# Two 64-row query matmuls side by side in the array, with slots that alternate between two blocks

## The chip, the core and the metric

The kernel runs on one core of a Trainium2 chip. The metric is the device time of one launch in microseconds (us), as the median of several runs. The core has a matmul engine (TensorE, PE in the profile; its weight loads have a row of their own, PEld), a vector engine (VectorE, DVE), an activation engine (ScalarE, ACT), a general engine (GpSimd, POOL), and a queue engine (SyncE, SP), which here issues all DMAs of the main loop. Matmuls write into PSUM, which this kernel uses as eight banks of 128 partitions by 512 fp32 columns; its other on-chip tiles lie in SBUF.

## What is computed

A transformer block on 2048 rows of 576 channels. Only the attention half touches the change:

```python
h = _layernorm(x) * (1 + ca) + sa
q = (h @ wq).reshape(B, Sq, 32, 128)          # 32 query heads
k, v = last 512 rows of the caches             # 16 key heads, each serves 2 query heads
scores = einsum("bhqd,bhkd->bhqk", q, k) * 128 ** -0.5
o = einsum("bhqk,bhkd->bhqd", softmax(scores), v)
x = x + ga * (o.reshape(B, Sq, 4096) @ wo)
...                                            # then a gated MLP of width 4608
```

`ca`, `sa` and `ga` come from a small conditioning vector. The MLP half follows the attention half on the same rows.

## The kernel before, in words

**Numbers.** Every fp32 operand of a matmul is split into an fp16 high part and an fp16 low part, and a product is the sum of three matmuls: high by high, high by low, low by high.

**Query projection.** The 576 channels are four chunks of 128 and a rest of 64. For a block of 512 rows, `hT` holds nine slices of 128 by 512: the high parts of the four chunks, the low parts of the four chunks, and in slice `2*DC` the rest, its high part in partitions 0 to 63 and its low part in partitions 64 to 127 (`modulate` writes it; GpSimd makes the low rows). The weights of the rest stand twice, one copy for each half of the partitions. So `project` needs 14 matmuls of 128 by 128 by 512: three for each chunk (line 410), and two for the rest (line 414), the high weights over all 128 rows and the low weights over all 128 rows. Of the second one only the 64 rows with the high part of `hT` matter; the other 64 add low by low.

**Slots.** The attention work is 128 slots. A slot is one query head of one block of 512 rows: `u` is the use of a key head, `j` which of its two query heads, `b` the block. Each key head is used once over all four blocks (8 slots), or twice over two blocks (4 slots each), its split operands being stored and read back. Inside a use the slots went block by block: `(b0, j0), (b0, j1), (b1, j0), (b1, j1)`.

**Order.** The program is written out by hand: each engine's queue holds its instructions in the order of the code, and nothing reorders them. A slot has four steps `t`, one for each 128 rows. In each step TensorE does the scores of the slot (three matmuls, line 483), a third of the *next* slot's query projection (`query(i + 1, t)` for t = 0, 1, 2), and one piece of the output projection (`attend_out`, six matmuls of 288 columns, line 433). After the last step come twelve matmuls for the values of the slot before (line 562). Once per slot four 128 by 128 transposes turn one tile of the softmax (line 523); the other three tiles are turned by DMA. VectorE takes the row maximum of the scores (line 487), ScalarE the exponentials (line 500) and the high halves, GpSimd the low halves. Tasks for other slots (loading, scaling and splitting the next head's weights, normalizing a block, MLP weights) are hung onto steps with `at` and `step_at`; `R` is the first step of a use.

**Output projection.** A pair of slots `(j0, j1)` of one block accumulates in PSUM tile `E`, and VectorE adds the result to the block (line 590). The eight pieces of a pair go one to a step.

**PSUM.** Tag `A` has two banks that the queries `pq` and the value sums `po` take in turn, tag `S` two for scores, `E` takes two, and tag `T` two for transposes.

Of the kernel before, what the change touches and what calls it, by code (L numbers as in the profile page):

```python
# [48 lines left out]
def tile_block(  # L49
# [30 lines left out]

    E = psum.tile([P, 2, 512], F32, tag="E", name="pe", bufs=1)
    turning = ExitStack()
    tpool = turning.enter_context(tc.tile_pool(name="tpool", bufs=2, space=PSUM))

    def t_bank():
        return tpool.tile([P, 512], F32, tag="T", name="pt")

    def half_split(a):
        return a.rearrange("p (a n) -> p a n", a=2)
# [145 lines left out]

    def turn_rows(b, m, tag):

        ps = t_bank() if tag == "T" else bank(tag, "ps_n")
        for t in range(ST):
            nc.tensor.transpose(ps[:, t * P : (t + 1) * P], norms[b][1][t][:, m * P : (m + 1) * P], ident)  # L240
        return ps

    def modulate(hT, m, ps, shift, gain, on_vector=False):

        g, s = gain[:, m : m + 1], shift[:, m : m + 1]
        hf = pool.tile([P, SB], F32, tag="hf", name="hf", bufs=HF)
        high = hT[:, m if m < DC else 2 * DC, :]
        if on_vector:
            nc.vector.tensor_scalar(hf, ps, g, s, op0=ALU.mult, op1=ALU.add)
        else:  # L250
            nc.scalar.activation(hf, ps, AF.Identity, bias=s, scale=g)
        nc.gpsimd.tensor_copy(high, hf)
        if m < DC:
            nc.gpsimd.tensor_sub(hT[:, DC + m, :], hf, high)  # L254
        else:
            nc.gpsimd.tensor_sub(high[DR:], hf[DR:], high[DR:])  # L256

    def modulate_first(hT, turned, shift, gain):

# [168 lines left out]
    def back(o, w, t, first, last):  # L428

        rows = slice(t * P, (t + 1) * P)  # L430
        for n, (x, y) in enumerate(((0, 0), (0, 1), (1, 0))):
            for h in range(2):
# [5 lines left out]
                    stop=last and n == 2,  # L438
                )

    QP = (range(0, 5), range(5, 10), range(10, 14))

# [1 line left out]
    uses = [(g, (p, p + 1), p == 0) for p in (0, 2) for g in range(FIRST)]  # L446
    uses += [(g, tuple(range(NSB)), True) for g in range(FIRST, HKV - TAIL)]
    uses += [(g, (p, p + 1), p == 0) for p in (0, 2) for g in range(HKV - TAIL, HKV)]
    slots = [(u, j, b) for u, (_, blocks, _) in enumerate(uses) for b in blocks for j in range(2)]
    begins = [next(i for i, slot in enumerate(slots) if slot[0] == u) for u in range(len(uses))]  # L450
    n = len(slots)
    state = [dict() for _ in range(n)]
# [2 lines left out]
    def query(i, part):  # L455
        u, j, b = slots[i]
        st = state[i]
        if part == 0 or i == 0:
            st["q"] = bank("A", "pq") if i else E[:, 0, :]
        ps = st["q"]  # L460
        if i == 0:
            project_first(ps, wqs[u, j], hT[b])
        else:
            project(ps, wqs[u, j], hT[b], QP[part])
        if part == len(QP) - 1:
            q = st["qT"] = pool.tile([P, 2, SB], F16, tag=("qh", "ql")[i % 2], name="qT", bufs=QB)
            nc.scalar.activation(q[:, 0], ps, AF.Copy, scale=Q_DOWN)
            if not i:
                query_low(i)
# [84 lines left out]
    def values(i):  # L554
        u, j, b = slots[i]
        st = state[i]
        v = vals[u]
        pt = st["pt"]
        po = bank("A", "po")
        for c in range(KC):  # L560
            for n, (x, y) in enumerate(((0, 0), (1, 0), (0, 1))):
                nc.tensor.matmul(  # L562
                    po, v[:, x, c, :], pt[:, y, c, :], start=c == 0 and n == 0, stop=c == KC - 1 and n == 2
                )
        st["po"] = po
# [16 lines left out]
        nc.gpsimd.tensor_sub(o[:, 1, :], on, o[:, 0, :])  # L582

    def attend_out(pair, t, j, total):
        u, _, b = slots[2 * pair]
        back(state[2 * pair + j]["o"], wos[u][:, j], t, j == 0, j == 1)
        if j == 1:
            run(*total)
            a = half_split(acc[b][:, t, :])
            nc.vector.scalar_tensor_tensor(  # L590
                a, E[:, :, :HALF], factors[:, uses[u][0], 2:3], a, op0=ALU.mult, op1=ALU.add
            )


    outs = {}
    for pair in range(n // 2):
        for k in range(2 * ST):
            if pair < n // 2 - 2:
                when = divmod((2 * pair + 4) * ST + 2 + k, ST)
            elif pair < n // 2 - 1:  # L600
                when = (n, 2 + k // 4)
            else:
                when = (n + 1, 1 + k // 3)
            outs.setdefault(when, []).append((pair, *divmod(k, 2)))

# [14 lines left out]
    def store_h(b, m, tag, tag_out):  # L622

        if m == 0:
            hd[b] = dram.tile([D, SB], F32, name=f"h{b}")
        n = P if m < DC else DR
        ps = turn_rows(b, m, tag)
        hf = pool.tile([P, SB], F32, tag=tag_out, name="hf", bufs=RB if tag_out == "raw" else HF)
        nc.scalar.activation(
            hf, ps, AF.Identity, bias=vecs["shift", "b"][:, m : m + 1], scale=vecs["gain", "b"][:, m : m + 1]  # L630
        )
        store_later(hd[b][m * P : m * P + n, :], hf[:n], ("s", b, m) if tag == "T" else None)

    def combine_tiles(pair):

# [354 lines left out]
    def mlp():  # L990

        for g in range(len(groups)):
# [12 lines left out]
                act_steps(g, -1)  # L1005
            for k, name in enumerate(ORDER):
                if name == "p1":
                    st["y"] = bank("A", "py")
                elif name in ("p2", "p7"):
                    st["x"] = bank("S", "px")  # L1010
                product(
# [242 lines left out]
    def step_at(step, task, *args):  # L1254
        at(step // ST, step % ST, task, *args)

    again = {g for g, _, whole in uses if not whole}
    for u, (g, blocks, whole) in enumerate(uses):
        R = ST * begins[u]
        if not whole:  # L1260
            step_at(R - 10, load_made, "k", u, keys)
            step_at(R - 9, load_made, "w", u, wqs, 0)
            step_at(R - 8, load_made, "w", u, wqs, 1)
            step_at(R - 5, load_made, "v", u, vals)
            step_at(R + 5, load_made, "o", u, wos)
            continue
        if u:
            A = dict(load=-22, keys=-17, wq=-13, total=-9, scale=-9, put=-8, turn=-5, vals=-1)
            if u == 1:
                A.update(load=-16, keys=-13, wq=-13)  # L1270
            A = {k: R + v for k, v in A.items()}
            step_at(A["load"], load, keys, u, load_kv, k_cache, g)
            for j in range(2):
                step_at(A["load"] + 3 + j if u > 1 else A["load"], load, wqs, (u, j), load_in, wq, 2 * g + j)
                step_at(A["wq"] + 2 * j, find, wqs, u, j, j)
                step_at(A["put"] + 4 * j, put_in, u, j)
            step_at(A["load"] + 2, load, vals, u, load_kv, v_cache, g)
            step_at(A["keys"], find, keys, u, 2)
            step_at(A["keys"] + 2, find, vals, u, 3)
            step_sum(A["total"], totals, taken, u, 0, 4)  # L1280
            step_at(A["scale"], find_scales, u, 0, 4)
            step_at(A["turn"] - 1, put_keys, u)
            step_at(A["turn"], put_keys_low, u)
            step_at(A["vals"] - 1, put_values, u)
            step_at(A["vals"], put_values_low, u)
            step_at(R - 1, load, wos, u, load_out, g)
        step_at(R + 3 if u else 9, find, wos, u, 4)
        step_sum(R + 5 if u else 11, totals, taken, u, 4, 5)
        step_at(R + 7 if u else 11, find_scales, u, 4, 5)
        for j in range(2):  # L1290
            step_at(R + 5 + j if u else 9 + j, gate_out, u, j)
            step_at(R + 11 + 2 * j if u else 12 + 2 * j, put_out, u, j)
        if g in again:
            K = max(R - 2, 5)
            step_at(K, keep_made, "k", u, keys)
            step_at(K, keep_made, "w", u, wqs, 0)
            step_at(K + 2, keep_made, "w", u, wqs, 1)
            step_at(K + 3, keep_made, "v", u, vals)
            step_at(R + 15, keep_made, "o", u, wos)


    last_group = len(groups) - 1
# [93 lines left out]
    def begin_h(b):  # L1396
        hT[b] = new_h()

    def make_h(b, m, on_vector=False):
        modulate(hT[b], m, turn_rows(b, m, "T"), vecs["shift", "a"], vecs["gain", "a"], on_vector)  # L1400

    def statistics(i, b, steps):
        for t in range(ST):
# [10 lines left out]
            statistics(i + 2 * k, b + k, 2)  # L1414
    for i, b in ((7, 2), (9, 3), (111, 0), (111, 1)):
        at(i, -1, norm_root, b)
    for i, b in ((7, 2), (10, 3)):
        norm(i, b)
        at(i + 1, 0, begin_h, b)
        for m in range(DC + 1):  # L1420
            at(i + 1 + m // 3, m % 3, make_h, b, m)


    parts = {}
# [9 lines left out]

    for b, i in ((0, 111), (1, 114)):
        norm(i, b)
        for m in range(DC + 1):
            at(i + 1 + m // 3, m % 3, store_h, b, m, "T", "raw")
            step_at(ST * (i + 1 + m // 3) + m % 3 + 1, store_now, ("s", b, m))
    at(117, -1, begin_parts, 0)  # L1440
    for c in range(3):
        i = 117 + 3 * c
# [12 lines left out]
    for b, g in ((2, 6), (3, 9)):  # L1455
# [1 line left out]
        for t in range(ST):  # L1457
            at(("m", g), t, norm_rows, b, t)
        for m in range(DC + 1):
            at(("m", g + 1 + m // 3), 2 * (m % 3), store_h, b, m, "AS"[m % 2], "raw")  # L1460
    at(("m", 12), -1, begin_parts, 1)
    for c in range(3):
        g = 12 + 6 * c
# [25 lines left out]
    at(106, 2, make_cols, "shift", "b", 3, 0.0, "T")  # L1489
    at(109, 2, make_cols, "gain", "b", 4, 1.0, "T")  # L1490
    at(109, 3, lambda: spread_peaks("b", mlp_small))
    at(110, 1, lambda: scale_cols("b", t_bank(), mlp_small, 2.0**-8))
    at(n - 3, 1, act_factors, 0, (NF - FEW) // 2)
    for b in (2, 3):
        for t in range(ST):
# [17 lines left out]
    norm_shifts(0)  # L1513
    for t in (0, 2, 1, 3):
        norm_rows(0, t)
    turned = [turn_rows(0, m, "TTAAS"[m]) for m in range(DC + 1)]
    for m in range(DC + 1):
        weigh_col(wms[0], 0, m, m < 2)
    for k, key in enumerate((wqs[0, 0], wqs[0, 1], keys[0])):
# [30 lines left out]
        at(0, t // 2, norm_rows, 1, t)  # L1550
    at(0, 2, begin_h, 1)
    for m in range(DC + 1):
        at(*((0, 2), (0, 3), (1, -1), (1, 0), (1, 1))[m], make_h, 1, m, m % 2 == 1)
    for d, step in enumerate((5, 6, 7, 4, 5)):
        step_at(step, weigh, 2, d)

# [122 lines left out]
```

## Time and profile before

| | |
|---|---|
| three runs | 2770.61 us (median), 2769.95, 2776.88 |
| profiled execution | 2773.59 us, span 2771.7 us |
| attention slots 0 to 127 | from 33.1 us; the last slot starts at 1577.4 us |
| TensorE busy | 2692.8 us (97%) |
| VectorE, ScalarE, GpSimd busy | 1999.8, 1617.5, 1881.9 us |

The span is the time from the first to the last instruction of that one execution; the remaining 1.9 us lie around it. A matmul's row in the trace gives its start and a modelled end, which lies behind the start of the next matmul, since they overlap in the pipeline; so what a matmul costs in a stream is the distance between two starts, and not its duration.

### The profile page before, as it was taken

Reading aid. Unit: us, or ns where it says so; the run is one execution under the profiler, and the core shown is the slowest. Engines: PE = TensorE matmul, PEld = TensorE weight load, DVE = VectorE, ACT = ScalarE, POOL = GpSimd, SP = SyncE. Lnnn points to the kernel's source line nnn. Section 1 sums busy time; section 2 is a strip of 40 time slices with the busy share of each in tenths; the row PEclk is TensorE's granted clock in tenths of the full one; section 3 lists DMA queues with packets and bytes.
Section 4 is the critical chain, followed back from the end, with each engine's and each line's share of the span. In section 5 each row is a group of like instructions: output and inputs, shape, how many; then the busy total and the mean of one; then the engine's idle time right before and its main releaser. Section 6 shows DMA issues by size and latency. Waiting matters only on the chain.

```text
span 2771.7 us, 44752 instructions
## 1 busy us (share of the span) xinstructions
PE 2692.8 (97%) x15406; PEld 1515.9 (55%) x15406; DVE 1999.8 (72%) x3555; ACT 1617.5 (58%) x3013; POOL 1881.9 (68%) x1748
## 2 busy tenths in 40 slices
PE   6899999999999999999999999999999999999998
PEld 3455555555555555555555555555555555555554
DVE  7877787877788787877876667777776666666666
ACT  5777778777777778787677634544443333333332
POOL 5578788888788877777669537688873465333435
PEclk8999999999999999999999999999999999999999
DMA  5778888788787788979889935656643434333332
GB/s 184 174 174 195 196 177 192 169 184 192 160 185 167 191 186 201 206 182 213 184 190 223 239 112 171 200 170 199 213 135 108 160 121 128 104 103 111 104 110 78
DMA packets 593460, 463.84 MB, mean 167 GB/s; under 512 B 442704, under 2 KB 472528, under 8 KB 592208
## 3 DMA queue, kind: packets, MB, share of 16 engines
q1 hardware_dynamic: 592944, 460.69, 64.9%
q8 instruction: 121, 1.98, 0.3%
q14 instruction: 107, 0.88, 0.1%
q10 hardware_dynamic: 288, 0.30, 0.0%
HBM read 264.19 MB, written 95.99 MB: 130 GB/s over the span
## 4 chain that ended last, share of the span: by engine, by line
PE 52%; DVE 2%; issue 1%; ACT 1%; POOL 1%; DMA 0%; SPq 0%; DVEq 0%; ACTq 0%; POOLq 0%
PE py L847 15%; PE px L847 11%; PE pe L932 7%; PE pf L932 7%; PE pe L433 3%; PE po L562 3%; PE pss L483 3%; PE pq L410 2%; PE pt L523 0%; PE pq L414 0%; DVE table L487 0%; DVE acc L590 0%; DVE on L571 0%; DMA r<-row 0%; ACT p L500 0%
## 5 line engine op out<-in xcount | busy, mean ns | idle before, releaser
L537 POOL TENSOR_TENSOR hp<-p,hp 128x512 f16<-128x512 f32 x384 | 450.2, 1175 | 271.0 <-ACT hp L532 147.9
L500 ACT ACTIVATE p<-pss,table,factors 128x512 f32<-128x512 f32 x512 | 396.9, 775 | 360.9 <-DVE table L488 186.6
L847 PEld LDWEIGHTS <-wset 128*128 128x128 f16 x3528 | 344.6, 98 | 337.9 <-issue 5.3
L487 DVE TENSOR_REDUCE table<-pss 128x1 f32<-128x512 f32 x512 | 350.3, 684 | 209.9 <-PE pss L483 205.9
L847 PE MATMUL py<-hset,wset 128*128 128x512 f16 x2016 | 483.6, 380 | 0.0
L433 PE MATMUL pe<-o 128*128 128x288 f16 x3072 | 459.6, 286 | 15.8 <-DVE acc L590 15.3
L483 PE MATMUL pss<-k,qT 128*128 128x512 f16 x1536 | 420.1, 381 | 13.7 <-ACT p L500 10.3
L433 PEld LDWEIGHTS <-o 128*128 128x128 f16 x3072 | 300.7, 98 | 189.6 <-issue 22.4
L562 PE MATMUL po<-ptw,v 128*128 128x512 f16 x1536 | 359.3, 382 | 10.4 <-DVE ptw L552 5.5
L847 PE MATMUL px<-hset,wset 128*128 128x512 f16 x1512 | 361.6, 379 | 1.6 <-ACT p L500 1.6
L410 PE MATMUL pq<-hT,wq 128*128 128x512 f16 x1092 | 283.2, 382 | 1.0 <-POOL hT L254 0.7
L94 POOL TENSOR_TENSOR akv<-u,akv 128x512 f16<-128x512 f32 x141 | 165.0, 1180 | 174.3 <-ACT akv L93 166.5
L532 ACT CAST hp<-p 128x512 f16<-128x512 f32 x384 | 237.3, 618 | 13.2 <-POOL hT L256 0.6
L562 PEld LDWEIGHTS <-v 128*128 128x128 f16 x1536 | 148.2, 98 | 175.4 <-issue 19.4
L932 PEld LDWEIGHTS <-akv 128*128 128x128 f16 x1728 | 169.6, 98 | 93.8 <-issue 4.8
L483 PEld LDWEIGHTS <-qT 128*128 128x128 f16 x1536 | 147.9, 98 | 129.0 <-issue 15.6
L590 DVE SCALAR_TENSOR_TENSOR acc<-pe,factors,acc 128x576 f32<-128x576 f32 x256 | 207.7, 811 | 10.4 <-PE pe L433 10.4
L582 POOL TENSOR_TENSOR o<-on,o 128x512 f16<-128x512 f32 x128 | 150.4, 1175 | 55.6 <-ACT o L581 52.7
L410 PEld LDWEIGHTS <-wq 128*128 128x128 f16 x1092 | 107.5, 98 | 129.7 <-issue 4.6
L926 DVE SCALAR_TENSOR_TENSOR acc<-pf,table,acc 128x576 f32<-128x576 f32 x140 | 113.4, 810 | 80.3 <-PE pf L932 80.3
L1027 ACT COPY u<-py 128x512 f32<-128x512 f32 x72 | 42.2, 586 | 202.1 <-PE py L847 200.2
L1020 ACT ACTIVATE s<-s,table 128x512 f32<-128x512 f32 x72 | 52.0, 722 | 173.9 <-DVE s L1019 173.9
(244 smaller groups left out, 4791.2 us busy)
## 6 DMA issues: line engine op xcount, KB each, us to landing
wset<-wd SPq DMA_DIRECT2D x213, 320.0 KB, 3.2
r<-row SPq DMA_DIRECT2D x128, 256.0 KB, 3.9
oset<-od SPq DMA_DIRECT2D x106, 288.0 KB, 3.2
wraw<-in_w SPq DMA_DIRECT2D x36, 768.0 KB, 5.7
wd<-wmade SPq DMA_DIRECT2D x75, 320.0 KB, 3.3
wset<-wd SPq DMA_DIRECT2D x71, 160.0 KB, 2.3
w2raw<-in_w SPq DMA_DIRECT2D x19, 576.0 KB, 5.3
wd<-ring SPq DMA_DIRECT2D x33, 320.0 KB, 2.8
```

The lines of the kernel that those rows point to most:

```text
L94: eng.tensor_sub(halves[:, 1], src, halves[:, 0])
L410: nc.tensor.matmul(ps, w[:, k // 2, m, :], hT[:, DC + m if k == 1 else m, :], start=s == 0, stop=False)
L433: nc.tensor.matmul(E[:, h, :HALF], o[:, x, rows], w[:, y, h * HALF : (h + 1) * HALF], start=first and n == 0, stop=last and n == 2,)
L483: nc.tensor.matmul(pss, q[:, x, rows], k[:, y, :], start=n == 0, stop=n == 2)
L487: nc.vector.tensor_reduce(nm[:, 0:1], pss, axis=AX.X, op=ALU.max, negate=True)
L500: nc.scalar.activation(p, pss, AF.Exp, bias=nm[:, 1:2], scale=factor, accum_out=st["l"][:, t : t + 1])
L532: nc.scalar.copy(hp[:, 0, :], state[i]["p", t])
L537: nc.gpsimd.tensor_sub(hp[:, 1, :], state[i].pop(("p", t)), hp[:, 0, :])
L562: nc.tensor.matmul(po, v[:, x, c, :], pt[:, y, c, :], start=c == 0 and n == 0, stop=c == KC - 1 and n == 2)
L590: nc.vector.scalar_tensor_tensor(a, E[:, :, :HALF], factors[:, uses[u][0], 2:3], a, op0=ALU.mult, op1=ALU.add)
L847: nc.tensor.matmul(ps, w[:, a, :], h[:, b, :], start=start and n == 0, stop=stop and n == 6, skip_group_check=True)
L932: nc.tensor.matmul(ps[:, h, :HALF], a[:, rows], w[:, b, :], start=m == 0, stop=m == 2)
```

## The change

The slots of a use now alternate between two blocks, `(b0, j0), (b1, j0), (b0, j1), (b1, j1)`, except in the first and the last use. So two consecutive slots, an even one and the odd one behind it, share the query head, and with it the weights. Blocks with odd numbers keep the low part of the rest in partitions 0 to 63 and the high part in 64 to 127, the other way round than even blocks. At the first step of the even slot's projection stand two matmuls of 64 rows: low weights, rows 0 to 63, with the even block's high part, into the even slot's bank; and low weights, rows 64 to 127, with the odd block's high part, into the odd slot's bank. Each of the two projections then needs 13 more matmuls. Queries get two banks of their own (tag `Q`); the value sums get one (tag `A`), and transposes keep one (tag `T`). The tasks that use `T` are placed anew and some go to `A`. The output projection of a pair now takes slots `i` and `i + 2`, and starts one slot later; loading and scaling the output weights moves back by 4 to 8 steps.

```diff
-    tpool = turning.enter_context(tc.tile_pool(name="tpool", bufs=2, space=PSUM))
+    tpool = turning.enter_context(tc.tile_pool(name="tpool", bufs=1, space=PSUM))
...
-            nc.gpsimd.tensor_sub(high[DR:], hf[DR:], high[DR:])
+            nc.gpsimd.tensor_sub(high[low], hf[low], high[low])
...
+    def project_paired(ps, w, hT, steps):
+        for s in steps:
+            m, k = divmod(s, 3)
+            if m < DC:
+                nc.tensor.matmul(
+                    ps, w[:, k // 2, m, :], hT[:, DC + m if k == 1 else m, :], start=False, stop=False
+                )
+            else:
+                nc.tensor.matmul(ps, w[:, 0, DC, :], hT[:, 2 * DC, :], start=False, stop=True)
...
+    PAIRED = (range(0, 4), range(4, 9), range(9, 13)), (range(0, 5), range(5, 9), range(9, 13))
...
+            quad = [(u, j, b) for j in range(2) for b in two]
+            slots += quad if 0 < u < len(uses) - 1 else [quad[k] for k in (0, 2, 1, 3)]
...
         elif not paired[i]:
             project(ps, wqs[u, j], hT[b], QP[part])
         else:
+            if i % 2 == 0 and part == 0:
+                other = state[i + 1]["q"] = bank("Q", "pq")
+                for to, rows, block in ((ps, slice(0, DR), b), (other, slice(DR, P), slots[i + 1][2])):
+                    nc.tensor.matmul(
+                        to, wqs[u, j][rows, 1, DC, :], hT[block][rows, 2 * DC, :], start=True, stop=False
+                    )
+            project_paired(ps, wqs[u, j], hT[b], PAIRED[i % 2][part])
...
-        po = bank("A", "po")
+        po = t_bank("A")
...
+        both = (i - i % 4 + pair % 2, i - i % 4 + pair % 2 + 2) if paired[i] else (i, i + 1)
...
+            elif pair == n // 2 - 3:
+                when = divmod((n - 1) * ST + 2 + k // 2, ST)
             else:
-                when = (n + 1, 1 + k // 3)
+                when = divmod((i + (5 if paired[i] else 4)) * ST + 2 + k, ST)
...
-            step_at(R - 1, load, wos, u, load_out, g)
-        step_at(R + 3 if u else 9, find, wos, u, 4)
+            step_at(R + 7, load, wos, u, load_out, g)
+        step_at(R + 10 if u else 9, find, wos, u, 4)
...
+    TIMES = (0, 2, "T"), (0, 2, "A"), (0, 3, "T"), (1, 2, "T"), (1, 3, "T")
+    for i, b in ((8, 2), (10, 3)):
+        at(i, 2, begin_h, b)
+        for m, (slot, t, tag) in zip((DC, *range(DC)), TIMES):
+            at(i + slot, t, make_h, b, m, False, tag)
```

Three places show how TensorE's and SyncE's queues change. The names carry buffer numbers: `pq` is a query bank, `hT_378` and `hT_512` are blocks 0 and 1, `wq` the query weights. First, TensorE in slot 33, behind the third matmul of the first step's scores. Before:

```order
L483 MATMUL pss_5112<-k_4791,qT_5058 128x512
L410 LDWEIGHTS wq_4719
L410 MATMUL pq_5125<-hT_512,wq_4719 128x512
...
L410 MATMUL pq_5125<-hT_512,wq_4719 128x512
L414 LDWEIGHTS wq_4719
L414 MATMUL pq_5125<-hT_512,wq_4719 128x512
L414 LDWEIGHTS wq_4719
L414 MATMUL pq_5125<-hT_512,wq_4719 128x512
L433 LDWEIGHTS o_4806
```

and with the change:

```order
L508 MATMUL pss_5083<-k_4765,qT_5030 128x512
L486 LDWEIGHTS wq_4835
L486 MATMUL pq_5096<-hT_378,wq_4835 128x512
L486 LDWEIGHTS wq_4835
L486 MATMUL pq_5097<-hT_512,wq_4835 128x512
L446 LDWEIGHTS wq_4835
L446 MATMUL pq_5096<-hT_378,wq_4835 128x512
...
L446 MATMUL pq_5096<-hT_378,wq_4835 128x512
L450 LDWEIGHTS wq_4835
L450 MATMUL pq_5096<-hT_378,wq_4835 128x512
L433 LDWEIGHTS o_4780
```

The two matmuls of line 414 at the end of the projection become one (line 450), and two 64-row matmuls into two banks (line 486) stand at its head, once for two slots. In the whole program 254 matmuls of line 414 become 14, and 120 of line 450 and 120 of line 486 (60 pairs) appear.

Second, TensorE at the third step of slot 8, where the rows of block 2 are turned for its `hT` (line 240, `pt` is a transpose bank). Before:

```order
L414 MATMUL pq_1520<-hT_378,wq_1372 128x512
L433 LDWEIGHTS o_1316
L433 MATMUL pe_76<-o_1326,o_1316 128x288
...
L240 MATMUL pt_1622<-ident_71,xn_1382 128x128
L240 MATMUL pt_1622<-ident_71,xn_1385 128x128
L240 MATMUL pt_1622<-ident_71,xn_1428 128x128
L240 MATMUL pt_1622<-ident_71,xn_1463 128x128
L483 LDWEIGHTS qT_1449
```

and with the change:

```order
L450 MATMUL pq_1351<-hT_512,wq_1223 128x512
L240 MATMUL pt_1594<-ident_71,xn_1375 128x128
...
L240 MATMUL pt_1594<-ident_71,xn_1458 128x128
L240 MATMUL pt_1603<-ident_71,xn_1375 128x128
...
L240 MATMUL pt_1603<-ident_71,xn_1458 128x128
L508 LDWEIGHTS qT_1444
```

Two tiles are turned in this step now, one into the single bank of `T` and one into that of `A`, and no piece of the output projection stands ahead of them: the paired slots start their output projection one slot later, so four steps here have none, and the last slots have two pieces in a step instead.

Third, SyncE at the first use that goes over all four blocks (first slot 24), where the output weights are loaded (`oraw`). Before:

```order
L513 DMA r_4930<-row30_4883 128x512
L544 DMA_TRANSPOSE ptw_4900<-hp_4879 128x8x128
L349 DMA oraw_4953<-in_wo 128x1152
L544 DMA_TRANSPOSE ptw_4900<-hp_4911 128x8x128
L719 DMA od21_155<-omade_4897 128x576
L510 DMA row31_5018<-l_4840 128x4
```

and with the change:

```order
L535 DMA row32_5134<-l_4950 128x4
L749 DMA od23_157<-omade_5038 128x1152
L569 DMA_TRANSPOSE ptw_5149<-hp_5092 128x8x128
L538 DMA r_5180<-row32_5134 128x512
L569 DMA_TRANSPOSE ptw_5149<-hp_5130 128x8x128
L349 DMA oraw_5202<-in_wo 128x1152
L749 DMA wd6_116<-wmade_5110 128x1280
L569 DMA_TRANSPOSE ptw_5149<-hp_5160 128x8x128
```

The load stands two slots later, between the same kinds of neighbours.

## Prediction before the run

> **What bounds the kernel now.** I read the page first, then the busy times of the attention stage, the groups of TensorE by form, the timeline of one slot, and TensorE's waits in that stage.
>
> ```profile
> span 2771.7 us, 44752 instructions
> PE 2692.8 (97%) x15406; PEld 1515.9 (55%) x15406; DVE 1999.8 (72%) x3555; ACT 1617.5 (58%) x3013; POOL 1881.9 (68%) x1748
> 33.10:1577.40 1544.30, 1501.46 (x8526) 837.80 (x8527) 1195.16 (x2424) 1158.17 (x2246) 1213.36 (x1150) 0.99 0.82 186
> ```
>
> The third row is the attention stage; its columns are length, then busy time (and count) of PE, PEld, DVE, ACT, POOL, then granted clock and DMA. TensorE is busy for 97% of it, the next engine, GpSimd, for 79%. A slot without waits looks like this on TensorE:
>
> ```profile
> 712.59 0.59 PE L410 MATMUL pq<-hT,wq 128*128 128x512 f16 x2
> 713.02 0.59 PE L414 MATMUL pq<-hT,wq 128*128 128x512 f16 x2
> 713.45 0.90 PE L433 MATMUL pe<-o 128*128 128x288 f16 x6
> 714.19 0.81 PE L483 MATMUL pss<-k,qT 128*128 128x512 f16 x3
> ...
> 724.17 0.59 PE L410 MATMUL pq<-hT,wq 128*128 128x512 f16 x2
> ```
>
> Two matmuls of line 414 take from 713.02 to 713.45, so one takes 0.216 in the stream (0.43 / 2, and 0.65 / 3 for the scores). A piece of output projection takes 0.74. The slot takes 724.17 - 712.59 = 11.58 us, and that is 38 matmuls at 0.216 (8.21), four pieces at 0.74 (2.96) and four transposes: no idle time is left in it. So a matmul taken away here is taken off the path. What the stage loses beyond this are single waits:
>
> ```profile
> PE pe L433 <- DVE acc L590: 10.5, 10, 2.4
> PE pss L483 <- ACT p L500: 10.3, 15, 2.5
> PE po L562 <- DVE ptw L552: 5.5, 8, 2.9
> PE pq L414 <- POOL hT L256: 3.5, 1, 3.5
> PE pt L240 <- ACT hf L251: 2.1, 1, 2.1
> ```
>
> (total us, times, longest). They sum to 32 us in 1544, and none belongs to a resource that the change frees.
>
> **The matmuls taken away.** A pair of slots had four matmuls of line 414, 4 x 0.216. It now has two of them and a pair of 64-row matmuls. There are 60 such pairs (120 of the 128 slots). If the two halves overlap completely, a pair of slots saves up to 0.216, 60 x 0.216 = 13.0 us. What the halves cost is nowhere in the trace for 64 rows. The nearest thing is line 169, which twice uses the array in two halves of 64 columns, with full-size matmuls ahead and behind:
>
> ```profile
> 1363.07 0.25 PE L169 MATMUL pt<-ones,wm 128*128 128x1 f32 x1
> 1363.24 0.13 PEld L169 LDWEIGHTS pt<-ones,wm 128*64 128x64 f32 x1
> 1363.25 0.23 PE L169 MATMUL pt<-ones,wm 128*64 128x1 f32 x2
> 1363.46 0.20 PE L169 MATMUL pt<-ones,wm 128*64 128x1 f32 x1
> 1363.58 0.10 PEld L483 LDWEIGHTS <-qT 128*128 128x128 f16 x1
> 1363.59 0.39 PE L483 MATMUL pss<-k,qT 128*128 128x512 f16 x1
> ```
>
> These are the last full-size matmul, the first half-array weight load, the first two half-array matmuls, then the last half-array matmul, and the first full-size load and matmul behind it. Three things are to be seen. Two half-array matmuls fit into 0.23 where one takes 0.20, so the second starts within 0.03 of the first: halves do overlap at the start, and I charge 0.03 for the pair. On the way in, the new load starts at 1363.24, which is 0.08 before the modelled end of the old matmul (1363.07 + 0.25); on the way out at 1363.58, again 0.08 before the modelled end (1363.46 + 0.20). And the matmul starts 0.01 behind its load. In a normal stream the load runs ahead, with the matmul before:
>
> ```profile
> 712.59 0.10 PEld L410 LDWEIGHTS <-wq 128*128 128x128 f16 x1
> L414 PE MATMUL pq<-hT,wq 128*128 128x512 f16 x182 | 54.2, 379 | 3.5 <-POOL hT L256 3.5
> ```
>
> (the first matmul of line 410 also starts at 712.59, and its duration is the 0.379 that line 414's row shows.) So I read the switch as: the first load of the other shape waits until the array is nearly empty.
>
> **The price of a switch.** A matmul of 512 columns has its modelled end 0.379 behind its start. The load then starts at 0.379 - 0.08 = 0.30, its matmul at 0.31, where the stream would have gone on at 0.216: 0.094 lost. A pair of slots has two switches, in behind the scores' third matmul, out ahead of the next full projection matmul; on the way out the matmul takes 0.39 and not 0.38, 0.01 more for weights that come late. Sum for a pair of slots: 0.094 + 0.216 + 0.03 + 0.094 + 0.01 = 0.444, against 2 x 0.216 = 0.432 for the two matmuls replaced. That is +0.012, and 60 x 0.012 = **+0.7 us**: the gain is spent on the two switches.
>
> The bounds. From below: the same rows also allow that the load only waits for the previous load (1363.04 + 0.19 by the row below), which in the stream would long be over; then nothing is lost, and a pair saves 0.432 - 0.246 = 0.186, 60 x 0.186 = -11.2 us.
>
> ```profile
> 1363.04 0.19 PEld L169 LDWEIGHTS pt<-ones,wm 128*128 128x128 f32 x1
> 1362.73 0.47 PE L169 MATMUL pt<-ones,wm 128*128 128x1 f32 x3
> ```
>
> From above: the load waits for the modelled end, and its matmul for the whole load of 0.10: 0.379 + 0.10 - 0.216 = 0.263 a switch, 0.526 + 0.246 - 0.432 = 0.340 a pair, +20.4 us. I take the value in the middle, since the three full-size matmuls of the second row stand about 0.11 apart ((0.47 - 0.25) / 2) while each of their loads lasts 0.19, so a load as such doesn't wait for the previous one to end; what ends together with the wait, at both switches, is the matmul.
>
> The Trainium skill, "TensorE: Matmul & The Clock Gate", Part 3 (Packing small matmuls), gives the span of packed matmuls as one matmul plus about 4 ns for each further tile and names no cost of a switch; by it a pair would save 0.432 - 0.220, an estimate of -12.7 us in all. The same skill, "TensorEngine Tiling (Array Packing)", Tiling Modes, Key Properties, speaks against the change: changing the tiling mode, not just the tile, drains the engine. The 0.08 above agrees with that second rule twice; no row here shows a switch behind a 512-column matmul.
>
> **Order of slots, output projection.** All matmuls, maxima, exponentials and GpSimd subtractions of a slot stay, only for another block. The output projection's start moves back by one slot, so four steps in slots 8 and 9 have no piece and two later slots have double; 4 x 0.74 = 3.0 us of TensorE move from there to slots 127 and 128.
>
> ```profile
> 140.90:153.90 13.00, 13.00 (x79) 7.78 (x78) 11.75 (x24) 10.72 (x22) 10.31 (x12) 1.00 1.02 243
> 153.90:166.40 12.50, 12.50 (x76) 7.45 (x75) 9.40 (x21) 10.61 (x19) 9.09 (x10) 1.00 0.67 120
> ```
>
> In slots 8 and 9 VectorE is busy for 11.75 of 13.00, so slot 8 can't get shorter by more than about 1.3; at the end the full 3.0 are added where the MLP's matmuls already fill TensorE. Bounds 0 to +1.7, I take +0.5.
>
> **Banks.** The queries took every second bank of `A`, the value sums the other; with two and one of their own neither waits more. One bank for transposes is enough for the one tile a slot, which VectorE has read by the third step. The two blocks that are normalized early, and the two at slots 111 to 118, put ten more tiles through each pair of `T` and `A`; now each must wait for ScalarE's read of the one before. The row of line 240 above has one such wait of 2.1. Each new tile has at least a step, some 2.9 us, between; where two follow in one step they go to different banks. Bounds 0 and ten waits of 0.3, +3; I take +0.5. Block 3's rest, which was made five steps before its first reader, is now read two steps (5.8 us) behind: in slot 1, with one step, that cost the 3.5 of GpSimd's `hT`; I take +0.3 of 0 to 3.5.
>
> **Output weights.** They were loaded four steps before VectorE's maximum (line 305), now three.
>
> ```profile
> 339.27 0.58 SPq L349 DMA_DIRECT2D oraw<-in_wo  x1
> 347.72 1.34 DVE L305 TENSOR_REDUCE top<-oraw 128x1 bf16<-128x1152 f32 x1
> DMA to landing us min/median/max: 4.1/5.7/9.0
> 581.70 1.05 DVE L571 TENSOR_TENSOR on<-po,r 128x512 f32<-128x512 f32 x1 [2.95 <-DMA r<-row]
> 583.53 0.90 PE L433 MATMUL pe<-o 128*128 128x288 f16 x6 [2.44 <-DVE acc L590]
> ```
>
> The shortest distance is 347.72 - 339.27 = 8.45; less a step of 2.9 it is 5.55, just under the median landing of 5.7. Behind the waiting maximum stand the scores' maxima, and behind these the exponentials and TensorE's score banks; the last two rows show that a VectorE wait of 2.95 on a DMA costs TensorE 2.44. Most uses have two or three us more in hand. Bounds 0 and 15 loads x (9.0 - 5.55) x 2.44 / 2.95 = 43 us if every load were as slow as the slowest; near the median it is nothing, and I take +0.2. The other moved tasks (gates, splits on ScalarE and GpSimd) keep their distance to the first reader: it moved by a slot, too.
>
> **Sum.** 0.7 + 0.5 + 0.5 + 0.3 + 0.2 = +2.2 us on 2773.59, the profiled execution (span 2771.7 plus 1.9). That one lies 3.0 above the median of 2770.61, inside the three runs, so the forecast is 2770.6 + 2.2 = **2773 us**, no change. A measurement of this kernel can tell 0.3%, 8.3 us, from none.
>
> **Rivals.**
> *The switch is free.* The new load needs only the earlier load, and both halves stream together: -11.2 + 1.5 for the side costs, 2761 us. For it: the halves' starts within 0.03, and loads that run a whole matmul ahead everywhere else. Against it: 0.08 before the matmul's end, twice. It is decided by the loss of a switch: below 0.02 each, the kernel is faster by more than 8.3.
> *The switch empties the array completely.* The mechanism is the one of the forecast, with the load only behind the modelled end: between 0.163 (0.379 - 0.216) and 0.263 a switch, so +0.140 to +0.340 a pair, +8.4 to +20.4 us, and 2781 to 2793 with the side costs. For it: single-column matmuls can't show what 512 columns leave in the pipeline. Against it: the 0.08. From 0.162 a switch on, the kernel is slower by more than 8.3.
> *The halves don't overlap.* They start together, but one streams behind the other: 0.186 more for a pair, +11.2, 2784 us. For it: the half-array matmuls in the trace have one column, so nothing of their streaming is seen. If the switch were free as well, nothing at all would change, 2772.
>
> **Chances.** Forecast 0.50 (its own range 2768 to 2780), free switch 0.22, empty array 0.16, halves that don't overlap 0.06, half-free switches the rest, 0.06. Of the last I count 0.05 as faster: faster 0.27, slower 0.16 + 0.05 = 0.21, the rest within 0.3%, 0.52. The range reaches down to the free switch (2759) and up over the lower part of the other two (2785).
>
> **What the profile after would show.** The two line 486 matmuls start within 0.03 of each other, the first 0.31 behind the third score matmul before it, and the next projection matmul 0.31 behind the second; two undisturbed slots together take 2 x 11.58 us, within 0.02. At 0.22 and 0.22 the free switch is right (22.97 for two slots); at 0.38 or more the empty array; a matmul behind the pair at 0.52 means no overlap. Waits of line 240 on ScalarE and of line 305 on `oraw` stay under 1 us each. The forecast is wrong above all if a 512-column matmul leaves the array otherwise than a one-column one.

## The result, and the profile after

| | before | changed |
|---|---|---|
| median | 2771.71 us | 2801.57 us |
| profiled span | 2771.7 us | 2800.9 us |
| ratio | | 1.0101, 95% interval 1.0086 to 1.0117 |

The change makes the kernel 1.0% slower, some 28 us by the ratio (29.9 by the medians, 29.2 by the profiled spans), where no change was forecast. From the page of the changed kernel, with the attention stage in the third row:

```profile
span 2800.9 us, 44829 instructions
PE 2699.5 (96%) x15406; PEld 1506.6 (54%) x15406; DVE 2001.4 (71%) x3555; ACT 1618.8 (58%) x3013; POOL 1881.6 (67%) x1748
33.10:1605.10 1572.00, 1505.83 (x8502) 825.96 (x8503) 1195.09 (x2422) 1159.70 (x2246) 1213.61 (x1150) 0.99 0.81 183
```

The engines' work is the same to a few us. The attention stage is taken up to the start of the last slot, as in the prediction: 1572.0 us where it had 1544.3. So 27.7 of the 29 us are lost in attention. There TensorE's idle time (length less busy time) grew from 42.8 to 66.2 us and its busy time by 4.4. The busy time hides the start of each wait: a 512-column matmul counts as busy up to its modelled end, 0.379 behind its start, where in the stream the next one starts at 0.216, so a wait behind it shows only from 0.163 on.

First the place that the prediction was about, a pair of 64-row matmuls in slot 63 (PE, then its weight loads):

```profile
812.56 0.81 PE L508 MATMUL pss<-k,qT 128*128 128x512 f16 x3
813.31 0.39 PE L486 MATMUL pq<-hT,wq 64*128 64x512 f16 x2
813.63 1.04 PE L446 MATMUL pq<-hT,wq 128*128 128x512 f16 x4
...
813.30 0.10 PEld L486 LDWEIGHTS <-wq 64*128 64x128 f16 x2 [0.42 <-issue]
813.62 0.33 PEld L446 LDWEIGHTS <-wq 128*128 128x128 f16 x3 [0.23 <-issue]
```

Two half matmuls fit into 0.39, no longer than one takes (0.386): they overlap fully, 0.003 to 0.004 apart in the instructions' own start times. The third score matmul starts at 812.56 + 2 x 0.216 = 812.99, the pair 0.31 behind it, and the next full matmul 0.32 behind the pair. The brackets show the weight loads that no longer run ahead. Over all 60 pairs the distance from the last score matmul to the next projection matmul is 0.633 to 0.645, 0.634 in the median, and 0.011 more follow because the weights come late, against 3 x 0.216 = 0.648 before: at this place nothing is gained and nothing lost, as forecast.

The pairs do leave their mark on the slots. Line 450 ends the projection that runs in a slot:

```profile
819.43 0.38 PE L450 MATMUL pq<-hT,wq 128*128 128x512 f16 x1
...
830.84 0.38 PE L450 MATMUL pq<-hT,wq 128*128 128x512 f16 x1
```

Undisturbed slots are no longer 11.58 us each, but in turn 11.79 (the one with the pair) and 11.36 to 11.41 (here 830.84 - 819.43, with two short matmuls of another task in it), together 23.15 without such tasks.

Now the idle time. TensorE's longest waits in the attention stage after:

```profile
PE pt L587 <- DVE ptw L577: 10.7, 17, 2.9
PE pe L310 <- DVE top L305: 9.5, 13, 1.6
PE pss L508 <- ACT p L525: 9.5, 13, 2.3
PE pe L433 <- DVE acc L616: 8.5, 6, 3.4
PE pt L240 <- DVE ptw L577: 7.4, 8, 2.3
...
PE pt L169 <- issue: 1.7, 1, 1.7
PE pt L1107 <- DVE ptw L577: 1.4, 1, 1.4
...
PE pt L169 <- DVE ptw L577: 1.2, 1, 1.2
```

and the same two releasers before:

```profile
PE pe L310 <- DVE top L305: 0.5, 1, 0.5
...
PE pt L240 <- DVE ptw L552: 0.2, 1, 0.2
```

Lines 508 and 433 wait no longer than before. New are two waits that the kernel before hardly knew. One is line 310, TensorE's column sum of the output weights' peaks, for VectorE's maximum (0.5 to 9.5). The other is whatever goes into the single transpose bank (lines 240, 169, 1107), for VectorE's read of the softmax tile in it (0.2 to 11.7, with line 169's 1.7 that ends in the same place). The value matmuls' wait for VectorE grew from 5.5 to 10.7. (Counted from start to start, so with the part that the busy time hides, line 310 lost 11.6 us to VectorE and line 240 8.7; these are the numbers in the expectations of e1 and e2.)

How the first comes about is seen in slot 34, on TensorE and then on VectorE:

```profile
471.21 0.81 PE L508 MATMUL pss<-k,qT 128*128 128x512 f16 x3
471.86 0.90 PE L433 MATMUL pe<-o 128*128 128x288 f16 x6
473.57 0.16 PE L310 MATMUL pe<-top,peak_cols 128*128 128x1 bf16 x1 [0.82 <-DVE top L305]
...
471.58 0.68 DVE L577 TENSOR_TENSOR ptw<-pt,ptw 128x512 f16<-128x512 f32 x1
472.17 1.34 DVE L305 TENSOR_REDUCE top<-oraw 128x1 bf16<-128x1152 f32 x1
473.43 0.68 DVE L512 TENSOR_REDUCE table<-pss 128x1 f32<-128x512 f32 x1
```

The maximum is hung onto a slot's third step, the sum onto the fourth. In its third step VectorE first has the softmax tile (line 577). In its fourth step TensorE has no query projection: between the scores and the sum stand only six short matmuls, so it arrives early. And the second in slot 8, where two tiles for block 2 are turned:

```profile
146.93 0.38 PE L450 MATMUL pq<-hT,wq 128*128 128x512 f16 x1
149.48 1.06 PE L240 MATMUL pt<-ident,xn 128*128 128x128 f32 x8 [2.17 <-DVE ptw L577]
...
147.79 0.64 DVE L512 TENSOR_REDUCE table<-pss 128x1 f32<-128x512 f32 x1
148.47 0.21 DVE L513 TENSOR_SCALAR table<-table,factors 128x1 f32<-128x1 f32 x1
148.64 0.69 DVE L577 TENSOR_TENSOR ptw<-pt,ptw 128x512 f16<-128x512 f32 x1
```

The tile of line 240 needs the bank that VectorE reads with line 577 in the *same* step, behind the row maximum. TensorE stands still until that read ends.

### The profile page after: what moved, and what is told of

Read it like the earlier page. It is cut to its first block, busy times and chain, and to the rows that moved or that the text cites. A ratio compares the mean times of both kernels' runs of the same rounds, so it can differ in the third digit from the quotient of the medians.

```text
span 2800.9 us, 44829 instructions
## 1 busy us (share of the span) xinstructions
PE 2699.5 (96%) x15406; PEld 1506.6 (54%) x15406; DVE 2001.4 (71%) x3555; ACT 1618.8 (58%) x3013; POOL 1881.6 (67%) x1748
## 5 line engine op out<-in xcount | busy, mean ns | idle before, releaser
L587 PE MATMUL pt<-ptw,v 128*128 128x512 f16 x1536 | 358.7, 381 | 14.9 <-DVE ptw L577 10.7
L446 PE MATMUL pq<-hT,wq 128*128 128x512 f16 x1056 | 271.5, 379 | 0.0
L446 PEld LDWEIGHTS <-wq 128*128 128x128 f16 x1056 | 99.7, 98 | 124.1 <-issue 10.0
```

The source lines that it names most:

```text
L446: nc.tensor.matmul(ps, w[:, k // 2, m, :], hT[:, DC + m if k == 1 else m, :], start=False, stop=False)
L587: nc.tensor.matmul(po, v[:, x, c, :], pt[:, y, c, :], start=c == 0 and n == 0, stop=c == KC - 1 and n == 2)
```

## The experiments

Theory A: the switch is neutral, and the loss is made of new waits around it. Theory B: the 64-row pairs themselves are the loss. Later a theory C: the new order of slots costs by itself. Every ratio is to executions of the kernel before that were taken beside that run (medians 2771.7 to 2774.0 us), so runs are compared by their ratios.

**e1, the sum later.**

```diff
-        step_sum(R + 11 if u else 11, totals, taken, u, 4, 5)
+        step_sum(R + 13 if u else 11, totals, taken, u, 4, 5)
```

> One edit of the changed kernel: TensorE's column sum of the output weights' peaks (line 310) stands at step R + 13 and no longer at R + 11, so three steps and not one behind VectorE's maximum (line 305), as far as its scales allow. Theory A (the loss is made of new waits; the switch of shapes costs nothing in sum): TensorE waited 11.6 us for that maximum over the whole trace, against 0.7 before, so the time falls by 9 to 12 us, to about 2791. Theory B (the loss comes with the 64-row pairs themselves): within 3 us of the changed kernel, 2801.

Measured: 2795.52 us, ratio to before 1.0079 (1.0066 to 1.0091), so 6 us less than the changed kernel. The wait of line 310 is gone; the waits of line 433 for VectorE grew by some 2 us. Less than forecast, but against B.

**e2, the extra tiles off the transpose bank.**

```diff
-    TIMES = (0, 2, "T"), (0, 2, "A"), (0, 3, "T"), (1, 2, "T"), (1, 3, "T")
+    TIMES = (0, 2, "A"), (0, 3, "T"), (1, -1, "T"), (1, 2, "A"), (1, 3, "T")
...
-    at(106, 2, make_cols, "shift", "b", 3, 0.0, "T")
+    at(106, 2, make_cols, "shift", "b", 3, 0.0, "A")
```

(and the same for the other two tasks of lines 169 and 1107)

> The changed kernel, with the extra tiles that were put into the single bank of T at the third step of a slot moved: at the third step they go to A's bank, into T only at the fourth step or at the slot's start. Theory A: TensorE's waits for VectorE's read of the softmax tile in that bank (8.7 us in line 240, 4.7 in lines 169 and 1107, against 0.2 before) go, so the time falls by 9 to 13 us, to about 2790. Theory B: within 3 us of 2801.

Measured: 2795.87 us, ratio 1.0084 (1.0070 to 1.0098), 5 to 6 us less. Only half of the gain, and the trace tells why:

```profile
PE pt L587 <- ACT hf L659: 2.5, 4, 1.0
PE pt L587 <- ACT hf L251: 2.3, 3, 1.4
...
PE pt L240 <- DVE ptw L577: 1.1, 1, 1.1
```

Line 240's wait fell from 7.4 to 1.1, but the tile now stands in the bank of the value sums, and the value matmuls at the slot's end wait for ScalarE to read it. In both places that were tried, the one bank of its kind was still in use.

**e3, both edits.**

> Both edits, the sum moved and the tiles moved. Theory A: the two gains add up, 18 to 25 us, to 2777 to 2784; what is left above the kernel before is the longer wait of the value matmuls for VectorE (5.5 us more than before). Theory B: still about 2800.

Measured: 2789.27 us, ratio 1.0054 (1.0040 to 1.0068): 12 to 13 us less than the changed kernel, about the sum of e1 and e2, and short of the forecast. In its trace the value matmuls wait 11.9 us for VectorE and 5.9 for ScalarE's read of the tiles, where the changed kernel had 10.7 and nothing.

**e4, full-size query matmuls.**

```diff
-        elif not paired[i]:
+        elif True:
             project(ps, wqs[u, j], hT[b], QP[part])
```

> The changed kernel with its slot order, its banks and all moved tasks, but every query projection with 14 full-size matmuls again; only the 64-row pairs are gone. Theory A: the pair and its two switches cost 0.633 us where two full matmuls and the one ahead take 0.648, so the time stays within 3 us of 2801. Theory B: the pairs are the loss, and the time falls to that of the kernel before, about 2772.

Measured: 2795.09 us, ratio 1.0085 (1.0070 to 1.0099). Against the changed kernel's 1.0101 that is 0.16%, some 4 us, where A expected at most 3 and B 29. B has fallen: of the 1.0%, 0.85% stay without any 64-row matmul. That the pairs aren't quite free either is suggested and not shown, since the two intervals overlap.

**e5, the second gate multiplication in a first step** (on top of e3).

```diff
-            step_at(R + 12 + j if u else 9 + j, gate_out, u, j)
+            step_at(R + 12 + 4 * j if u else 9 + j, gate_out, u, j)
```

> Both edits of e3, and VectorE's second multiplication of the output weights by the gate moved from step R + 13, where VectorE also normalizes a slot, to R + 16, the first step of the next slot. Theory A says that what e3 still loses is value matmuls that wait for a late VectorE (11.9 us in the attention stage, 5.5 before); this takes 0.9 us of VectorE out of the slot where the wait recurs in every use of eight slots: 2 to 5 us less than e3. A rival, that these waits come from DMAs or from ScalarE: no change against e3.

Measured: 2782.81 us, ratio 1.0041 (1.0028 to 1.0054). That is 0.13% or 4 us less than e3, as forecast, and the wait of the value matmuls for VectorE fell from 11.9 to 8.2. But the intervals of e3 and e5 overlap, and the two profiled executions are equally long (2787.5 and 2787.4 us): in e5's, the scores' wait for ScalarE's `qT` grew from 1.1 to 3.5. The gain is not shown.

**e6, a gap of one step in the kernel before.**

```diff
-        step_at(R + 3 if u else 9, find, wos, u, 4)
+        step_at(R + 4 if u else 9, find, wos, u, 4)
```

> The kernel before with one number changed: VectorE's maximum of the output weights stands at step R + 4 instead of R + 3, so one step ahead of TensorE's sum and not two, as in the changed kernel. Nothing else of the change. Theory A: TensorE waits for it in most of the 15 uses, 8 to 12 us more than before, about 2783. If the wait was only the meeting of all moved tasks: under 3 us more.

Measured: 2768.93 us, ratio 0.9988 (0.9980 to 0.9997). A miss: one step between maximum and sum costs nothing between a slot's first and second step. Line 310 waits 0.5 us there, as before. So it isn't the distance alone. (This kernel, one number away from the kernel before, is the fastest of all here, by 0.1%.)

**f1, the same gap between the third and the fourth step.** The kernel before with

```diff
-        step_at(R + 3 if u else 9, find, wos, u, 4)
+        step_at(R + 6 if u else 9, find, wos, u, 4)
-        step_sum(R + 5 if u else 11, totals, taken, u, 4, 5)
+        step_sum(R + 7 if u else 11, totals, taken, u, 4, 5)
```

and the gates at R + 8 and R + 9.

> The kernel before, with VectorE's maximum of the output weights at R + 6 and TensorE's sum at R + 7 (the third and the fourth step of a slot, one step apart, as R + 10 and R + 11 in the changed kernel), and the two gate multiplications moved behind, to R + 8 and R + 9. e6 showed that one step apart is harmless between the first and the second step. If it is the fourth step that matters, which has no query projection on TensorE, behind a third step in which VectorE also has the softmax tile: 7 to 11 us more than before, 2781. If not: within 3 us of before.

Measured: 2779.73 us, ratio 1.0029 (1.0018 to 1.0040), 8 us more than before, with nothing else of the change. The wait is the one of the changed kernel:

```profile
PE pe L310 <- DVE top L305: 9.2, 8, 2.6
```

So the place is the cause: the maximum in the third step, the sum in the fourth. Which of the two steps matters more, f1 doesn't tell. The gates moved as well here; f2 below moves them to R + 8 and R + 12 without loss. The profiled execution is the fastest of seven (2775.96 us): line 310 waits 8.7 us more in it than before, and other waits are shorter, so its span is only 2.4 us longer.

**e7, full-size matmuls and the old banks** (against e4).

```diff
-    tpool = turning.enter_context(tc.tile_pool(name="tpool", bufs=1, space=PSUM))
+    tpool = turning.enter_context(tc.tile_pool(name="tpool", bufs=2, space=PSUM))
...
-        return psum.tile([P, 512], F32, tag=tag, name=name)
+        return psum.tile([P, 512], F32, tag="A" if tag == "Q" else tag, name=name)
...
-        po = t_bank("A")
+        po = bank("A", "po")
```

> As e4 (slot order and moved tasks of the changed kernel, full-size query matmuls), with the banks of the kernel before: queries and values take two banks in turn, transposes have two. Against e4 only the banks differ. Theory A: the waits of lines 240, 169 and 1107 for VectorE's read of the single bank go, 9 to 13 us less than e4's 2795, about 2784. Theory C (it is the new order of slots that costs, whatever the banks): as e4.

Measured: 2782.91 us, ratio 1.0037 (1.0023 to 1.0051) against e4's 1.0085: 13 us. The banks alone are nearly half of the loss. The single-bank waits shrank, from 10.4 us in e4 (lines 240, 169 and 1107) to 2.4, and what e4 had of line 310's stayed:

```profile
PE pe L310 <- DVE top L305: 7.3, 8, 1.6
...
PE pt L240 <- DVE ptw L577: 2.4, 2, 1.5
```

**g1, the order alone.** e7 with the sum at R + 13 and the second gate at R + 16, so neither pairs nor fewer banks nor the sum in the fourth step.

> e7 (slot order and moved tasks of the changed kernel, full-size query matmuls, banks of the kernel before) with the sum at R + 13 and the second gate multiplication at R + 16. What is left of the change is the alternating order of the slots, the output projection one slot later, and tasks at other steps. If the bank, the sum and the pairs are the whole loss: within 4 us of the kernel before, 2773. If the order costs by itself: 8 us more, 2781 or above.

Measured: 2776.84 us, ratio 1.0011 (1.0002 to 1.0020). Theory C is worth 3 us (0.6 to 5.5 by the interval), with the tasks that moved in it.

**e8, e3 with full-size matmuls.**

> As e3 (sum moved, tiles moved), with full-size query matmuls in place of the 64-row pairs. Theory A with a switch that costs nothing: within 3 us of e3, 2789. If the unequal slots that the pairs make (11.36 and 11.79 us where all had 11.58) uncover waits, as e4 against the changed kernel suggests: 4 to 7 us less, 2784.

Measured: 2780.86 us, ratio 1.0032 (1.0020 to 1.0045), against e3's 1.0054: 6 us less. Again the kernel with pairs is 4 to 6 us slower, which their own matmuls don't show. The intervals touch here, too; two comparisons with the same sign make a cost of the pairs likely.

**f3, equal slots.** e5, and one full matmul of the even slot's projection moved into the fourth step of the lighter slot ahead:

```diff
+    def query_early(i):
+        u, j, b = slots[i]
+        st = state[i]
+        st["q"] = bank("Q", "pq")
+        st["early"] = True
+        nc.tensor.matmul(st["q"], wqs[u, j][:, 0, 0, :], hT[b][:, 0, :], start=True, stop=False)
...
+            if t == ST - 1 and i % 2 == 0 and 4 < i + 2 < n and paired[i + 2]:
+                query_early(i + 2)
```

> e5 (paired; sum, tiles and second gate moved), with one full matmul of an even slot's projection issued a slot earlier, in the fourth step of the lighter slot. So all slots take the same 11.58 us of TensorE, and the fourth step has one matmul more ahead of the value matmuls. If the unequal slots are what the pairs cost (e4 and e8 were 6 and 8 us below their paired partners): 4 to 7 us less than e5, about 2777. If the pairs cost in another way: within 2 us of e5, 2783.

Measured: 2781.89 us, ratio 1.0032 (1.0020 to 1.0043), e5 had 1.0041 (1.0028 to 1.0054). Inconclusive: the change has the forecast sign, the slots are all 11.58, and the value matmuls' wait for VectorE fell from 8.2 to 6.5, but the medians differ by 1 us and the intervals overlap. That the unequal slots are what the pairs cost is not shown: the measured 1 to 3 us lie between the two forecasts.

**f2, e6 with the gates in first steps, too.** (R + 8 and R + 12 in place of R + 5 and R + 6.)

> The kernel before as in e6 (maximum at R + 4, the first step of a slot), and the two gate multiplications at R + 8 and R + 12, first steps, too, instead of R + 5 and R + 6, second and third. If VectorE's extra work costs least in the first step of a slot, where it has no tile, no normalization and no query half: 1 to 4 us less than e6, about 2766. If e6's gain was chance: as before, 2772.

Measured: 2770.20 us, ratio 0.9992 (0.9983 to 1.0001). A miss: nothing gained over e6.

**f4, the halves apart.** Each slot's 64-row matmul at the head of its own projection, alone:

```diff
-            if i % 2 == 0 and part == 0:
-                other = state[i + 1]["q"] = bank("Q", "pq")
...
+            if part == 0:
+                rows = slice(DR, P) if i % 2 else slice(0, DR)
+                nc.tensor.matmul(
+                    ps, wqs[u, j][rows, 1, DC, :], hT[b][rows, 2 * DC, :], start=True, stop=False
+                )
```

> The changed kernel with the two 64-row matmuls of a pair apart, each at the head of its own slot's projection, so 120 times into the other shape and out again with one matmul each, and no overlap. By the trace of the changed kernel a half alone costs 0.311 + 0.318 + 0.011 - 0.216 = 0.424 us, a pair of slots 0.848 in place of 0.428: 60 x 0.42 = 25 us more than the changed kernel, about 2826. If the slots have slack where the switches fall, or waits move under them: 15 to 20 more.

Measured: 2812.85 us, ratio 1.0145 (1.0131 to 1.0159), 11 to 12 us more than the changed kernel and not 25. In undisturbed slots the forecast price is there: every slot takes 11.79 us, two of them 23.58 against 23.15. But in slots where TensorE waited anyway, the 0.2 us of two more switches only took the place of waiting: over the attention stage TensorE's busy time is 23.8 us longer than in the changed kernel (1529.6 against 1505.8), and its idle time 12.9 shorter (53.3 against 66.2).

## Why the prediction was wrong

**What held.** TensorE bounds the stage, and a switch to half rows waits until the array is nearly empty (the new load starts 0.07 before the old matmul's modelled end): 0.31 in, 0.32 out, the halves 0.003 to 0.004 apart. The sum for a pair was forecast at +0.012 us, and by the starts it is 0.634 + 0.011 - 0.648 = -0.003; most of the difference is the second half's start, charged at 0.03. This term, taken from two switches behind one-column matmuls, was right for 512 columns. The Trainium skill's "TensorEngine Tiling (Array Packing)", Tiling Modes, Key Properties, states that a change of the tiling mode drains the engine. The trace agrees in every one of the 60 pairs: the first half starts 0.311 to 0.323 behind the last full matmul and not 0.216. The Trainium skill's "TensorE: Matmul & The Clock Gate", Part 3, gives about 4 ns for each further tile and names no cost of a switch. The trace agrees on the tiles (3 to 4 ns); a sum by it alone would have missed the switch. The range failed on what the prediction priced as side costs, and the measured time lies above every rival, too, whose highest was 2793.

**Banks: +0.5 us forecast, some 13 measured (e4 against e7).** The step that failed: "Each new tile has at least a step, some 2.9 us, between; where two follow in one step they go to different banks." It looked at ScalarE's read of the tile before. The bank is also read by VectorE, for the softmax tile, behind the row maximum of every slot's third step; the prediction had it that VectorE "has read by the third step". Into just that step and that bank went two of the five tiles of each block, and the tasks at slots 106, 109 and 110. How late the read comes stood in the trace before, in the slot that the prediction shows:

```profile
715.01 0.69 DVE L552 TENSOR_TENSOR ptw<-pt,ptw 128x512 f16<-128x512 f32 x1 [1.13 <-ACT ptw L527]
```

TensorE was through with its third step at 714.19 there (the row of line 483), and VectorE with the bank at 715.70, 1.5 us later. Eight tiles at that price would be 12 us, an estimate from this one slot; line 240 lost 7.4 by its row. The row of line 240 that was quoted named ScalarE alone, and the sign that the prediction gave for this term, line 240's wait on ScalarE, hardly moved (2.1 before, 3.0 after). The other releaser, VectorE's `ptw`, was in the trace with 0.2 us, because the second bank hid it. A wait that a second buffer covers stands in the profile at nothing; its price has to be taken from the distance between the two instructions in the step.

**Output weights: +0.2 forecast, 7 to 8 measured (f1; e7 against g1, with the gate).** The step that failed: the prediction followed the load's landing to VectorE's maximum and stopped there: "The other moved tasks ... keep their distance to the first reader". The sum of line 310 didn't: the maximum moved by 7 steps, the sum by 6. That distance is harmless in the first and second step (e6) and costs in the third and fourth (f1), and there the pair stands, since 7 is no multiple of 4.

**Order of slots: +0.5 forecast, 3 measured (g1, 0.6 to 5.5),** above the term's own bound of 1.7, though g1 also holds the tasks that moved.

**Pairs beyond their own matmuls: not in the prediction, likely 4 to 6 us (changed kernel against e4, e3 against e8).** The prediction checked that two slots together take 23.16. That one of them becomes shorter by 0.2, so that waits which 11.58 had just covered may show, was not asked. Between e4 and the changed kernel several rows grew by 1 to 2 us each (the value matmuls' for VectorE and for DMAs, line 310's, the scores' for ScalarE); f3 left it open whether the unequal slots are the cause.

Taken off one after another, from 1.0101 the pairs take 0.16% (e4), the banks 0.48% (e7), the sum and the gate 0.26% (g1), and 0.11% stay for the order. These shares add up by construction; in the other order, the sum alone took 0.22% (e1) and the pairs 0.22% (e8). The prediction's list of TensorE's waits (32 us of 42.8 idle) stopped above the two rows, 0.5 and 0.2, that grew. The rivals were all about the switch; the one that decided, a bank that becomes the bound, was not among them, so the chance of 0.21 for slower came from the wrong places.

## What to carry to other kernels

Half-array matmuls in a stream of full-size ones pay for the way in and the way out, here 0.2 us together, about what one saved 512-column matmul brings. By these figures a second pair behind the same switch would bring its 0.21 us whole, an estimate: no run here has one. When a change takes a buffer from another use, list *every* reader of what is left and the step in which it reads, for a covered wait shows nothing in the profile before. And when tasks move by a number of steps, check producer against consumer one by one, and in which step of the slot they land: a gap of one step cost nothing in one place and some 8 us in another.

## What the runs showed of the hardware

A weight load for another array shape starts 0.071 to 0.072 before the modelled end of the last matmul of the old shape, whether that has one column or 512, and whether the array is halved by columns (before) or by rows (after). In the next row of the changed kernel, columns are least, median and greatest duration in ns:

```profile
L486 PE MATMUL pq<-hT,wq x88: 386/386/387, 79.5 to 1271.5; 64*128 64x512 f16 x88
```

A half-row matmul takes the same time as a full one (0.386, against 0.379 for a full one whose weights ran ahead and 0.389 to 0.390 for the full one right behind each pair, whose weights come late as well), so 64 rows save nothing but through overlap.
